# Folding the fourth and fifth modulation vector onto 64 partitions, with one matmul each

## The chip, the cores and the metric

The kernel runs on one core of a Trainium2 chip. A core has a matrix engine (PE, TensorE) with its own weight loads (PEld), a vector engine (DVE, VectorE), an activation engine (ACT, ScalarE), a general engine (POOL, GpSimd) and a queue for transfers (SP, SyncE). Each works through its own list of instructions in the order in which the program wrote them; semaphores make one engine wait for another. The metric is the time of one execution on the device in microseconds. Before the change it was 435.3 us, the median of three runs (435.18 to 435.45).

## What is computed

A block with adaptive layer norm: six modulation vectors of 448 numbers come from one small product, and shift, scale and gate a linear attention and a token-mixing MLP. Shapes: S = 2048 tokens, D = 448 channels, F = 1792, 16 heads of 28.

```python
mod = (_silu(c) @ w_mod).reshape(c.shape[0], 6, 1, -1)
sa, ca, ga, sb, cb, gb = (mod[:, 0], mod[:, 1], mod[:, 2], mod[:, 3], mod[:, 4], mod[:, 5])
h = _layernorm(x, axis=-1) * (1 + ca) + sa
x = x + ga * _A_ref(h, A_wqkv, A_wo)        # linear attention: phi(q), sums of phi(k) v, divided by den
h = _layernorm(x, axis=-1) * (1 + cb) + sb
x = x + gb * _B_ref(h, B_w1, B_b1, B_w2, B_b2)   # MLP over the token axis
```

The fourth vector is `sb`, the shift of the second layer norm (number 3 in the code, which counts from 0), the fifth is `cb`, its scale (number 4). Both are needed from the second stage on only.

## The kernel before

The 2048 tokens are 16 tiles of 128. In the first stage (the loop over `t` at L674) each tile gets its projection to keys, `phi` of it (`pk`), a copy of the normalised input (`xn`, split into a high half `xh` on ACT and a low half `xl` on DVE), and products of both that PE adds up in four banks (`cacc`). Numbers of full precision go through PE as a high and a low half, so most products are three matmuls; the high half is a copy on ACT, the low half a subtraction on DVE that waits for it (`split`, L83). Behind the loop the sums are closed: `zp` from the summed `pk` (L784), `csum` (`cs`, L794 to L796) from `cacc`, `kvb` from that and the value weights (L805), `kvm` (L809), then `wp` (L955), which PE multiplies from `kvm`. The second stage (L975) runs over the tiles once more: the transposes `tq` of the normalised queries `pn` are its first work on PE, and later `b_norm1_a` and `b_norm1_b` (L905, L909) read the fifth and the fourth vector. Pieces of the MLP's weights are loaded all along (`pr`, L316) and split into `ph` (ACT) and `pl` (DVE), two or four at a time, by `split_to` at places written out by hand. The schedule is manual: each engine gets its instructions in the order of the code.

A modulation vector is made from four blocks of `w_mod` with 112 rows each. `mod_part` (L228) scales one block by `silu(c)` and adds it to `acc`, a tile of 112 partitions by 448; what is left to do is the sum over the partitions, which is one product with ones on PE (`mod_sum2`, L256), whose result stands on all 128 partitions. `acc` has full precision, so it goes through PE in two halves. There are two ways: `split` makes two tiles of 112 partitions, `mh` and `ml`, and `mod_sum2` two matmuls; or, for the vectors named in `FOLDED`, `halves` (L236) first adds partitions 64 to 111 to 0 to 47, so that 64 are left, and then puts the high half on partitions 0 to 63 and the low half on 64 to 127 of one tile, for which one matmul does. The third and sixth vector are folded; the fourth and fifth go the first way, in `mod_split(4)` and `mod_split(3)` at L787 and L788, right behind `zb`. Their matmuls stand at L800, ahead of `kvb`, and at L811, behind it; `mod_out` copies the result to `mods`.

Of the kernel before, what the change touches and what calls it, by code (L numbers as in the profile page):

```python
# [8 lines left out]
F32 = mybir.dt.float32  # L9
# [9 lines left out]
G = 112  # L19
# [22 lines left out]
WARM = 6  # L42
POOL_LOW = (0, 2)
PRE = 9
FOLDED = (2, 5,)
MID = 5
NSLOT, NTOK = 74, 27
LOAD2, SPLIT2 = 12, 4
# [4 lines left out]
def block_kernel(ctx: ExitStack, tc: tile.TileContext, x, xt, wqkv, wo, w1, b1, w2, b2, c, wmod, wfirst, out):  # L53
    nc = tc.nc
# [22 lines left out]
    def moving(new, name, dt=F32R, parts=P):  # L77
        return new(name, dt=dt, parts=parts, w=512)[:, 16:16 + D]

    def bank(name):  # L80
        return psum.tile([P, 512], F32, name=name, tag="bank")

    def split(full, hi, lo):  # L83
        nc.scalar.activation(hi, full, AF.Copy)  # L84
        nc.vector.tensor_sub(lo, full, hi.bitcast(F32))  # L85
# [114 lines left out]
    mods, macc = {}, {}  # L200
# [32 lines left out]
            nc.vector.scalar_tensor_tensor(macc[j], wm[j, k], sc[:G, k:k + 1], macc[j], op0=ALU.mult, op1=ALU.add)  # L233


    def halves(acc, new, name):  # L236
        n = acc.shape[0] - 64
        nc.vector.tensor_add(acc[:n], acc[:n], acc[64:])
        both = moving(new, name)
        nc.scalar.activation(both[:64], acc[:64], AF.Copy)  # L240

        def low():
            nc.vector.tensor_sub(both[64:], acc[:64], both[:64].bitcast(F32))
        return both, low

    def mod_split(j):
        acc = macc.pop(j)
        if j in FOLDED:
            both, low = halves(acc, slot, f"mh{j}")
            low()  # L250
            macc[j] = (both,)
        else:
            macc[j] = (moving(slot, f"mh{j}", parts=G), moving(slot, f"ml{j}", parts=G))
            split(acc, *macc[j])

    def mod_sum2(j):  # L256
        ps = bank(f"modp{j}")
        part = macc.pop(j)
        for i, m in enumerate(part):
            nc.tensor.matmul(ps[:, :D], ones_r[:m.shape[0], :], m, start=(i == 0), stop=(i == len(part) - 1))  # L260
        return ps
# [28 lines left out]
    def row_sum(j):  # L290
        rowb[j] = bank(f"rowb{j}")
        ws = [Whi[j, ch] for ch in range(4)] + [Wlo[j, ch] for ch in range(3)]
        for i, w in enumerate(ws):
            nc.tensor.matmul(rowb[j][:ROWS, :D], sel_s, w, start=(i == 0), stop=False)

    def row_bias(j):
        nc.tensor.matmul(rowb[j][:ROWS, :D], sel_b, accb.pop(j), start=False, stop=True)
# [10 lines left out]
    raws, parts = {}, {}  # L308
# [17 lines left out]
    def split_to(i):  # L326
        while done["split"] < min(i, len(pieces)):
            k = done["split"]
            new = tslot if k in TOKP else slot
            hi, lo = new(f"ph{k}", dt=F32R, w=512), new(f"pl{k}", dt=F32R, w=512)  # L330
            if k in PIECE_DMA:
                full = raws.pop(k)
                nc.scalar.activation(hi, full, AF.Copy)
                nc.scalar.activation(lo, hi.bitcast(F32), AF.Copy, scale=-1.0)
                low_dma.append((lo, full))
            else:
                split(raws.pop(k), hi, lo)
            parts[k] = (hi, lo)
            done["split"] += 1
# [60 lines left out]
    def a_rows(t):  # L400
        g, r = groups.pop(t)[:, :, 0:2], rowst[t // 2 % RING].rearrange("p (t b c) -> p t b c", t=2, b=2)
        nc.vector.tensor_copy(r[:, :, :, 0:2], g.unsqueeze(2).to_broadcast([P, 2, 2, 2]))

        def low():
            nc.vector.tensor_sub(r[:, :, 0, 2:4], g, r[:, :, 0, 0:2].bitcast(F32))
        return low
# [6 lines left out]
    def a_copy(t):  # L413
        nc.scalar.activation(heads[t][1][64:ROWS, 384:], tps.pop(t), AF.Copy)
# [26 lines left out]
    def project(t, j, name):  # L441
        projects([(t, kind, ch) for ch in range(3) for kind in ("hh", "wl", "hl")] + [(t, "hh", 3)], j, name)

    def close(t, j):
        ps = pps.pop((t, j))
        nc.tensor.matmul(ps[:, :D], heads[t][1][:ROWS, 384:], Wrow[j][:ROWS], start=False, stop=True)  # L446
        return ps[:, :D]
# [23 lines left out]
    def phi_q(t):  # L471
        dst, (e, r) = slot(f"pq{t}"), eqs.pop(t)
        nc.vector.scalar_tensor_tensor(dst, e, 1.0, r, op0=ALU.min, op1=ALU.add)
        return dst
# [4 lines left out]
    def a_q(t):  # L479
        project(t, 0, "qp")  # L480
        qps[t] = close(t, 0)
        del heads[t]

    def a_exp_q(keep=0):
        for t in sorted(qps)[:len(qps) - keep]:
            q_exp(qps.pop(t), t)

    def a_phi_q(keep=0):
        a_exp_q(keep)
        for t in sorted(eqs):  # L490
            pq[t] = phi_q(t)
# [135 lines left out]
    low = a_rows(2)  # L627
# [18 lines left out]
    low = a_rows(4)  # L646
# [20 lines left out]
    low = a_rows(6)  # L667
# [6 lines left out]
    for t in range(4, NT):  # L674
        if 5 < t < NT - 1:
            project(t + 1, 1, "kp")
        kp = close(t, 1) if t > 4 else kps[4]
        if t == 9:
            row_sum(0)
            row_bias(0)  # L680
        if t > 4:
            a_outer(t - KV_LAG)
        if t % 2 and 4 < t < NT - 2:
            a_transpose(t + 1)
        if t in Q_EARLY:
            a_q(Q_EARLY[t])
        if t == 12:
            mp = mod_sum2(2)
        pair = t % 2 and 7 < t + 3 < NT
        if pair:  # L690
            first, second, end = a_stats_dve((t + 3, t + 4))
            first(0)
        if 5 <= t < 9:
            w_low(0, t - 5)
        if pair:
            second(0)
        if 5 <= t < 9:
            row_part(0, t - 5)
        a_phi_q(t in Q_EARLY)
        if t == 9:  # L700
            a_exp(t, kp)
        if t % 2 and 4 < t < NT - 2:
            a_copy(t + 1)
            a_copy(t + 2)
        if t != 9:
            a_exp(t, kp)
        if 7 < t + 3 < NT:
            a_split_high(t + 3)
        a_pk_parts(t - 1)
        highs = HIGH_AT.get(t, (t - 2,))  # L710
        for i in highs[:1]:
            a_norm(i)
            a_high(i)
        if t % 2 == 0 and 4 < t < NT - 3:
            low = a_rows(t + 2)
        a_pk(t, kp)
        if t % 2 == 0 and 4 < t < NT - 3:
            low()
        if 7 < t + 3 < NT:
            a_split_low(t + 3)  # L720
        for i in highs[1:]:
            a_norm(i)
            a_high(i)
        if pair:
            first(1)
        for i in highs:
            a_low(i)
        if pair:
            second(1)
            end()  # L730
        sum_end()
        if 4 <= t < 8:
            w_high(0, t - 4)
            if t == 7:
                w_row(0)
        if t == 9:
            row_out(0)
        if t == 12:
            mod_out(2, mp)
            make_mask()  # L740
        if t in FETCH:
            load_xt(FETCH[t])
            load_x(FETCH[t])
        if 7 <= t < 11:
            mod_part(2, t - 7)
        if t == 11:
            mod_split(2)
        for j, i in MOD_AT.get(t, ()):
            mod_part(j, i)
        if t in (7, 10):  # L750
            load_mod(4 if t == 7 else 3)
        if t == 10:
            load_qkv(2, tslot)
        if t == 8:
            for g in range(4):
                w = tslot(f"wo{g}", parts=G)
                nc.sync.dma_start(w, wo[g * G:(g + 1) * G, :])
                wo_sb.append(w)
            b1c = cst.tile([P, NF], F32, name="b1c")
            nc.sync.dma_start(b1c, b1)  # L760
            b2c = cst.tile([P, NT], F32, name="b2c")
            nc.sync.dma_start(b2c, b2)
        if t >= 13:
            nc.vector.tensor_mul(wo_sb[t - 13], wo_sb[t - 13], mods[2][:G])
        load_to(PRE_LOAD.get(t, 0))
# [18 lines left out]
        nc.tensor.matmul(zp[:, :D], ones_r, pk, start=(i == 0), stop=(i == 1))  # L784
    zb = tslot("zb")
    nc.scalar.activation(zb, zp[:, :D], AF.Copy, bias=S * 1e-6)
    mod_split(4)  # L787
    mod_split(3)  # L788
    load_to(14)
    split_to(4)  # L790
    a_q(late.pop(0))
    csum = []
    for ch in range(4):
        csum.append(slot(f"cs{ch}"))  # L794
        nc.scalar.activation(csum[ch], cacc[ch][:, :D], AF.Identity, scale=col[1][:, ch:ch + 1])
        nc.vector.scalar_tensor_tensor(csum[ch], zb, col[0][:, ch:ch + 1], csum[ch], op0=ALU.mult, op1=ALU.add)  # L796
    a_phi_q()
    a_q(late.pop(0))
    split_to(6)
    mp = mod_sum2(4)  # L800
    kvb = bank("kvb")
    for ch in range(4):
# [5 lines left out]
    kvm = slot("kvm", parts=G)  # L808
    nc.vector.tensor_mul(kvm, kvb[:G, :D], mask)  # L809
    mod_out(4, mp)  # L810
    mp = mod_sum2(3)  # L811
    load_to(PRE + MID + 3)
    split_to(8)
    Wpr, Wph, Wpl = [], [], []
# [133 lines left out]
            del parts[k]  # L948

    a_q(late.pop(0))  # L950
    for fn in (b_prod, b_sum, b_eps, b_recip, b_scale):
        fn(0)
    for g in range(4):
# [21 lines left out]
    for i in range(NT + LAG):  # L975
# [15 lines left out]
        t = i - LAG  # L991
# [9 lines left out]
        if i == NT:  # L1001
            mp = mod_sum2(5)
# [266 lines left out]
    for o0, n in W1G[1:]:  # L1269
# [5 lines left out]
        for r in range(first, NT):  # L1275
# [5 lines left out]
            if xleft:  # L1281
                t = xleft.pop(0)
# [81 lines left out]
```

## Time and profile before

| | |
|---|---|
| median of the runs | 435.3 us |
| the profiled execution, its own time | 435.4 us |
| its span, from first to last instruction | 433.7 us |
| granted clock of TensorE | 1.000 |
| last loop pass of the first stage, sums, start of the second stage | about 76 to 112 us |

All times below are microseconds from the start of the span. A timeline row has the start, the duration, the engine, the line, the operation, the output and inputs by their names in the program (without the tile's number), the shapes, the count of merged instructions and, in brackets, how long the engine was idle before it and what ended that. PE's matmuls overlap: their durations are longer than the distance from start to start, and it is that distance that counts.

### The profile page before, as it was taken

The page shows a single profiled execution, that of the slowest core. Times are in us where ns is not written, and L with a number is a line of the kernel's source. Part 1 is how long each engine was busy: PE and PEld are TensorE (multiplying, and loading weights), DVE is VectorE, ACT ScalarE, POOL GpSimd, SP SyncE. Part 2 cuts the span into 40 slices and gives each one's busy share as a digit, 9 for nine tenths or more (in the row PEclk, how much of TensorE's full clock was granted, in tenths as well). Part 3 has the DMA queues.
Part 4 walks back from the last instruction along what each step waited for, and adds up shares of the span by engine and source line. Part 5 has one row for each costly group of instructions (what it writes and reads, how often), then busy time and mean ns, then how long its engine had stood idle before and what let it go on. Part 6 is the DMA issues. An engine that isn't in the chain of part 4 may idle for free.

```text
span 433.7 us, 7208 instructions
## 1 busy us (share of the span) xinstructions
PE 428.1 (99%) x2333; PEld 395.5 (91%) x2333; DVE 362.2 (84%) x813; ACT 278.5 (64%) x595; POOL 119.6 (28%) x198
## 2 busy tenths in 40 slices
PE   8999999999999999999999999999999999999996
PEld 7788899999899989989999999999999999999996
DVE  4999987689799999996579695739799998898893
ACT  5899868658578799985855263537464664645550
POOL 2336444300025577775200000010113131122010
PEclk9999999999999999999999999999999999999999
DMA  8998996574200036345427461587479977886430
GB/s 278 384 334 179 242 249 152 107 225 164 86 1 0 26 73 148 73 98 121 147 85 241 144 212 50 167 209 201 85 181 215 228 157 153 218 176 125 82 54 32
DMA packets 63941, 66.14 MB, mean 152 GB/s; under 512 B 4960, under 2 KB 55456, under 8 KB 63904
## 3 DMA queue, kind: packets, MB, share of 16 engines
q1 hardware_dynamic: 54832, 50.90, 37.8%
q0 software_dynamic: 8784, 14.32, 21.1%
q10 hardware_dynamic: 288, 0.46, 0.5%
q8 instruction: 18, 0.29, 0.3%
q14 instruction: 19, 0.16, 0.1%
HBM read 46.30 MB, written 7.34 MB: 124 GB/s over the span
## 4 chain that ended last, share of the span: by engine, by line
PE 92%; DVE 4%; DMA 2%; issue 0%; POOL 0%; ACT 0%; SPq 0%; DVEq 0%
PE y L1159 19%; PE up L939 10%; PE up L938 10%; PE up L940 10%; PE y L1160 9%; PE cacc L551 8%; PE qp L439 7%; PE op L881 6%; PE kp L439 5%; PE tq L851 1%; PE op L888 1%; DMA wr<-in_qkv_dram 1%; DMA xt<-in_xt_dram 1%; PE qp L446 1%; PE kvb L805 1%; PE wp L955 1%
## 5 line engine op out<-in xcount | busy, mean ns | idle before, releaser
L939 PE MATMUL up<-h2l,ph 128*128 128x448 f32 x224 | 81.3, 363 | 0.0
L938 PE MATMUL up<-h2h,ph 128*128 128x448 f32 x224 | 81.2, 362 | 0.0
L940 PE MATMUL up<-h2h,pl 128*128 128x448 f32 x224 | 80.8, 361 | 0.0
L1114 POOL DMA_DIRECT2D a<-a x16 | 14.2, 962 | 137.8 <-DMA a<-in_B_w_dram 77.6
L938 PEld LDWEIGHTS up<-h2h,ph 128*128 128x128 f32 x224 | 42.0, 188 | 3.2
L940 PEld LDWEIGHTS up<-h2h,pl 128*128 128x128 f32 x224 | 41.9, 187 | 3.0
L939 PEld LDWEIGHTS up<-h2l,ph 128*128 128x128 f32 x224 | 42.0, 188 | 2.6 <-DVE h2l L935 0.3
L85 DVE TENSOR_TENSOR pl<-pr,ph 128x512 fp32r<-128x512 f32 x46 | 30.8, 688 | 4.1 <-ACT ph L84 3.3
L1165 ACT ACTIVATE cc<-y 128x448 f32<-128x448 f32 x24 | 13.0, 546 | 26.8 <-PE y L1160 26.8
L84 ACT ACTIVATE ph<-pr 128x512 fp32r<-128x512 f32 x46 | 27.6, 623 | 0.8 <-PE up L940 0.5
L1078 DVE TENSOR_TENSOR u<-u,mod 128x448 f32<-128x448 f32 x14 | 8.7, 623 | 21.7 <-ACT u L1077 21.5
L1077 ACT ACTIVATE u<-up,b1c 128x448 f32<-128x448 f32 x14 | 8.8, 625 | 24.1 <-PE up L940 23.5
L1179 POOL DMA_DIRECT2D out_dram<-yt x14 | 12.7, 908 | 40.8 <-DVE yt L1170 31.4
L439 PE MATMUL kp<-wh,hh 128*128 128x448 f32 x64 | 23.7, 375 | 0.0
L551 PE MATMUL cacc<-pkh,xh 128*128 128x448 f32 x64 | 23.6, 369 | 0.0
L439 PE MATMUL qp<-wh,hh 128*128 128x448 f32 x64 | 23.4, 366 | 0.0
L831 POOL TENSOR_SCALAR den<-den 128x16 f32<-128x16 f32 x16 | 8.8, 549 | 45.4 <-DVE den L828 45.4
L551 PE MATMUL cacc<-pkl,xh 128*128 128x448 f32 x56 | 20.3, 362 | 0.0
L881 PE MATMUL op<-wph,pth 128*128 128x448 f32 x48 | 18.7, 390 | 0.0
L1120 DVE TENSOR_TENSOR a<-a,s 128x512 f32<-128x512 f32 (+1 forms) x32 | 18.5, 622 | 0.0
L84 ACT ACTIVATE s2h<-s 128x512 fp32r<-128x512 f32 (+1 forms) x16 | 8.3, 569 | 15.5 <-DVE s L1120 15.5
L1159 PE MATMUL y<-ub,a11h 128*128 128x448 f32 x56 | 18.2, 375 | 0.0
(239 smaller groups left out, 1378.1 us busy)
## 6 DMA issues: line engine op xcount, KB each, us to landing
pr<-in_B_w_dram SPq DMA_DIRECT2D x56, 256.0 KB, 3.1
a<-in_B_w_dram SPq DMA_DIRECT2D x32, 256.0 KB, 4.4
a<-in_B_w_dram SPq DMA_DIRECT2D x32, 192.0 KB, 4.2
xt<-in_xt_dram SPq DMA_DIRECT2D x16, 256.0 KB, 5.0
x<-in_A_x_dram SPq DMA_DIRECT2D x16, 224.0 KB, 5.0
wm<-in_B_wmod_dram SPq DMA_DIRECT2D x16, 196.0 KB, 5.4
out_dram<-x SPq DMA_DIRECT2D x14, 224.0 KB, 2.2
out_dram<-yt POOLq DMA_DIRECT2D x14, 224.0 KB, 5.7
```

What stands on the lines that cost most here:

```text
L84: nc.scalar.activation(hi, full, AF.Copy)
L85: nc.vector.tensor_sub(lo, full, hi.bitcast(F32))
L439: nc.tensor.matmul(pps[t, j][:, :D], a[:, ch * P:(ch + 1) * P], w, start=first, stop=False)
L551: nc.tensor.matmul(cacc[ch][:, :D], a[:, s], b, start=(t == 0 and i == 0), stop=(t == NT - 1 and i == len(todo) - 1))
L881: nc.tensor.matmul(opb[t][:, :D], a, b, start=(ch == n == 0), stop=False)
L938: nc.tensor.matmul(ps[:, :D], hi[:, sl], mh, start=first, stop=False)
L939: nc.tensor.matmul(ps[:, :D], hi[:, sl], ml, start=False, stop=False)
L940: nc.tensor.matmul(ps[:, :D], lo[:, sl], mh, start=False, stop=last)
L1114: nc.gpsimd.dma_start(w, a, accum_op=ALU.add)
L1120: nc.vector.tensor_tensor(w, raw2[q, a][i], raw2[q, b][i], op=op)
L1159: nc.tensor.matmul(ps[:, :D], h[:, s], w, start=opens and r == 0, stop=False, skip_group_check=True)
L1160: nc.tensor.matmul(ps[:, :HD], l[:, s], wh, start=False, stop=closes and r == PAIRS - 1, skip_group_check=True)
```

## The change

Both vectors are folded now. `halves` is cut into three steps, `mod_add`, `mod_high` and a low half that is called by itself, so that they can stand at different places. For the fifth vector, add and high half are written at the end of tile 13 in the loop of the first stage, the low half at the end of tile 14; for the fourth the add stands behind `csum`, the high half behind the second projection there, and the low half behind the next pair of weight pieces. The fifth vector's sum stays ahead of `kvb`; the fourth's moves behind it and behind the next projection, ahead of `wp`.

```diff
-FOLDED = (2, 5,)
...
-    def halves(acc, new, name):
-        n = acc.shape[0] - 64
-        nc.vector.tensor_add(acc[:n], acc[:n], acc[64:])
-        both = moving(new, name)
+    def mod_add(j):
+        acc = macc[j]
+        nc.vector.tensor_add(acc[:G - 64], acc[:G - 64], acc[64:])
+
+    def mod_high(j):
+        acc, both = macc[j], moving(slot, f"mh{j}")
+        macc[j] = (both,)
         nc.scalar.activation(both[:64], acc[:64], AF.Copy)
-
-        def low():
-            nc.vector.tensor_sub(both[64:], acc[:64], both[:64].bitcast(F32))
-        return both, low
+        return lambda: nc.vector.tensor_sub(both[64:], acc[:64], both[:64].bitcast(F32))

     def mod_split(j):
-        acc = macc.pop(j)
-        if j in FOLDED:
-            both, low = halves(acc, slot, f"mh{j}")
-            low()
-            macc[j] = (both,)
-        else:
-            macc[j] = (moving(slot, f"mh{j}", parts=G), moving(slot, f"ml{j}", parts=G))
-            split(acc, *macc[j])
+        mod_add(j)
+        mod_high(j)()
...
+        if t == 13:
+            mod_add(4)
+            low4 = mod_high(4)
+        if t == 14:
+            low4()
...
-    mod_split(4)
-    mod_split(3)
     load_to(14)
     split_to(4)
     a_q(late.pop(0))
...
+    mod_add(3)
     a_phi_q()
     a_q(late.pop(0))
+    low3 = mod_high(3)
     split_to(6)
+    low3()
     mp = mod_sum2(4)
...
     mod_out(4, mp)
-    mp = mod_sum2(3)
...
     a_q(late.pop(0))
+    mp = mod_sum2(3)
     for fn in (b_prod, b_sum, b_eps, b_recip, b_scale):
```

Where the instructions stand, at the two places of which the prediction speaks. The lines of the changed kernel are other ones than before; in the names the number right behind the letters is the tile's, the vector's or the piece's, the one behind the underscore a running number.

ACT at the end of tile 13, before the change (`xh` of tiles 11 and 12, then the exponentials for the query of tile 3, `eq3`, and the key of tile 14):

```order
L503 ACTIVATE xh11_1169<-xn11_1167 128x448
L503 ACTIVATE xh12_1176<-xn12_1174 128x448
L468 ACTIVATE eq3_1222<-qp3_1138,mv2_334 128x448
L469 ACTIVATE rq3_1223<-qp3_1138,mv2_334 128x448
L453 ACTIVATE ek14_1228<-kp14_1113,mv14_993 128x448
L456 ACTIVATE rk14_1229<-kp14_1113,mv14_993 128x448
L519 ACTIVATE pkh13_1232<-pk13_1172 128x448
```

and now:

```order
L496 ACTIVATE xh11_1169<-xn11_1167 128x448
L496 ACTIVATE xh12_1176<-xn12_1174 128x448
L242 ACTIVATE mh4_1185<-acc4_872 64x448
L461 ACTIVATE eq3_1225<-qp3_1138,mv2_334 128x448
L462 ACTIVATE rq3_1226<-qp3_1138,mv2_334 128x448
L446 ACTIVATE ek14_1231<-kp14_1113,mv14_993 128x448
L449 ACTIVATE rk14_1232<-kp14_1113,mv14_993 128x448
L512 ACTIVATE pkh13_1235<-pk13_1172 128x448
```

The fifth vector's high half, `mh4`, stands between `xh12` and `eq3`, and everything behind it in the list comes after it. DVE at the same place, before (low halves of tiles 11 and 12, then the first part of the fourth vector):

```order
L509 TENSOR_TENSOR xl11_1170<-xn11_1167,xh11_1169 128x384
L508 TENSOR_TENSOR xh12_1176<-xn12_1174,xh12_1176 128x64
L509 TENSOR_TENSOR xl12_1177<-xn12_1174,xh12_1176 128x384
L231 TENSOR_SCALAR acc3_1184<-wm3_0_940,sc_194 112x448
L764 TENSOR_TENSOR wo0_784<-wo0_784,mod2_1107 112x448
L473 SCALAR_TENSOR_TENSOR pq3_1226<-eq3_1222,rq3_1223 128x448
L521 SCALAR_TENSOR_TENSOR pkl13_1233<-pk13_1172,pkh13_1232 128x448
```

and now:

```order
L502 TENSOR_TENSOR xl11_1170<-xn11_1167,xh11_1169 128x384
L501 TENSOR_TENSOR xh12_1176<-xn12_1174,xh12_1176 128x64
L502 TENSOR_TENSOR xl12_1177<-xn12_1174,xh12_1176 128x384
L237 TENSOR_TENSOR acc4_872<-acc4_872 48x448
L230 TENSOR_SCALAR acc3_1187<-wm3_0_940,sc_194 112x448
L762 TENSOR_TENSOR wo0_784<-wo0_784,mod2_1107 112x448
L466 SCALAR_TENSOR_TENSOR pq3_1229<-eq3_1225,rq3_1226 128x448
L514 SCALAR_TENSOR_TENSOR pkl13_1236<-pk13_1172,pkh13_1235 128x448
```

The add on `acc4` stands behind `xl12`; `mh4` on ACT reads its result. The low half of the fifth vector stands one tile later on DVE, behind `xl13`:

```order
L502 TENSOR_TENSOR xl13_1243<-xn13_1240,xh13_1242 128x384
L243 TENSOR_TENSOR mh4_1185<-acc4_872,mh4_1185 64x448
L232 SCALAR_TENSOR_TENSOR acc3_1187<-wm3_1_942,sc_194,acc3_1187 112x448
L762 TENSOR_TENSOR wo1_786<-wo1_786,mod2_1107 112x448
L466 SCALAR_TENSOR_TENSOR pq4_1272<-eq4_1268,rq4_1269 128x448
L514 SCALAR_TENSOR_TENSOR pkl14_1279<-pk14_1245,pkh14_1278 128x448
```

Before, `acc3` followed `xl13` there directly. Behind the sums, ACT before (from the exponentials of tile 5's query, over the third pair of weight pieces, to the copy of the fifth vector):

```order
L468 ACTIVATE eq5_1430<-qp5_1406,mv4_413 128x448
L469 ACTIVATE rq5_1431<-qp5_1406,mv4_413 128x448
L84 ACTIVATE ph4_1448<-pr4_1310 128x512
L84 ACTIVATE ph5_1452<-pr5_1312 128x512
L468 ACTIVATE eq6_1476<-qp6_1436,mv6_486 128x448
L469 ACTIVATE rq6_1477<-qp6_1436,mv6_486 128x448
L204 ACTIVATE mod4_1484<-modp4_1456 128x448
```

and now:

```order
L461 ACTIVATE eq5_1427<-qp5_1402,mv4_413 128x448
L462 ACTIVATE rq5_1428<-qp5_1402,mv4_413 128x448
L242 ACTIVATE mh3_1445<-acc3_1187 64x448
L83 ACTIVATE ph4_1447<-pr4_1314 128x512
L83 ACTIVATE ph5_1451<-pr5_1316 128x512
L461 ACTIVATE eq6_1475<-qp6_1433,mv6_486 128x448
L462 ACTIVATE rq6_1476<-qp6_1433,mv6_486 128x448
L203 ACTIVATE mod4_1483<-modp4_1456 128x448
```

The fourth vector's high half, `mh3`, stands ahead of the pieces `ph4` and `ph5`; before, both vectors had their high halves right behind `zb`, ahead of the second pair of pieces and of `csum`. DVE there before, from the two low halves that went with them to `pq6`, behind which comes `kvm`:

```order
L85 TENSOR_TENSOR ml4_1383<-acc4_872,mh4_1382 112x448
L85 TENSOR_TENSOR ml3_1387<-acc3_1184,mh3_1386 112x448
L85 TENSOR_TENSOR pl2_1399<-pr2_1296,ph2_1398 128x512
L85 TENSOR_TENSOR pl3_1403<-pr3_1298,ph3_1402 128x512
L796 SCALAR_TENSOR_TENSOR cs0_1418<-zb_1380,col0_199,cs0_1418 128x448
L796 SCALAR_TENSOR_TENSOR cs1_1421<-zb_1380,col0_199,cs1_1421 128x448
L796 SCALAR_TENSOR_TENSOR cs2_1424<-zb_1380,col0_199,cs2_1424 128x448
L796 SCALAR_TENSOR_TENSOR cs3_1427<-zb_1380,col0_199,cs3_1427 128x448
L473 SCALAR_TENSOR_TENSOR pq5_1434<-eq5_1430,rq5_1431 128x448
L85 TENSOR_TENSOR pl4_1449<-pr4_1310,ph4_1448 128x512
L85 TENSOR_TENSOR pl5_1453<-pr5_1312,ph5_1452 128x512
L473 SCALAR_TENSOR_TENSOR pq6_1480<-eq6_1476,rq6_1477 128x448
```

and now:

```order
L84 TENSOR_TENSOR pl2_1395<-pr2_1300,ph2_1394 128x512
L84 TENSOR_TENSOR pl3_1399<-pr3_1302,ph3_1398 128x512
L792 SCALAR_TENSOR_TENSOR cs0_1414<-zb_1384,col0_199,cs0_1414 128x448
L792 SCALAR_TENSOR_TENSOR cs1_1417<-zb_1384,col0_199,cs1_1417 128x448
L792 SCALAR_TENSOR_TENSOR cs2_1420<-zb_1384,col0_199,cs2_1420 128x448
L792 SCALAR_TENSOR_TENSOR cs3_1423<-zb_1384,col0_199,cs3_1423 128x448
L237 TENSOR_TENSOR acc3_1187<-acc3_1187 48x448
L466 SCALAR_TENSOR_TENSOR pq5_1431<-eq5_1427,rq5_1428 128x448
L84 TENSOR_TENSOR pl4_1448<-pr4_1314,ph4_1447 128x512
L84 TENSOR_TENSOR pl5_1452<-pr5_1316,ph5_1451 128x512
L243 TENSOR_TENSOR mh3_1445<-acc3_1187,mh3_1445 64x448
L466 SCALAR_TENSOR_TENSOR pq6_1479<-eq6_1475,rq6_1476 128x448
```

`ml4` and `ml3` are gone from ahead of `cs0`; the add on `acc3` stands behind `cs3`, and the low half, into `mh3`, behind `pl5`; `kvm` follows `pq6` as before.

## Prediction

> **What bounds the kernel now.** I read the page's busy times first, then the waits of PE (TensorE), then the windows around the two places that the change touches, then the timelines of PE, DVE (VectorE) and ACT (ScalarE) there.
>
> ```profile
> PE 428.1 (99%) x2333; PEld 395.5 (91%) x2333; DVE 362.2 (84%) x813; ACT 278.5 (64%) x595; POOL 119.6 (28%) x198
> ...
> PE warm L189 <- DVE roots L109: 1.1, 1, 1.1
> ...
> PE tq L851 <- DVE pn L838: 0.2, 1, 0.2
> ...
> 92.00:112.00 20.00, 20.00 (x112) 17.30 (x111) 18.56 (x34) 13.58 (x27) 0.29 (x1) 1.00 0.55 179
> 112.00:202.00 90.00, 89.72 (x471) 82.83 (x470) 82.90 (x196) 71.80 (x165) 51.91 (x95) 1.00 0.31 68
> ```
>
> PE is busy for 99% of the span, and its waits (total, times, longest) are some tenths of a microsecond behind the start-up. Nothing but PE sets the time, so a matmul less is worth its pitch and a microsecond for which PE stands still is a microsecond lost. The second window is the warning: from 92 to 112 us DVE is busy for 18.56 of 20 us (third figure behind PE and PEld). What is put on DVE there finds little idle time.
>
> **PE's own work.**
>
> ```profile
> 102.43 0.36 PE L260 MATMUL modp<-mh,ones_r 112*128 112x448 f32 x1
> 102.64 0.37 PE L260 MATMUL modp<-ml,ones_r 112*128 112x448 f32 x1
> 102.84 3.40 PE L805 MATMUL kvb<-cs,wr 128*112 128x112 f32 x32
> ...
> 106.49 0.37 PE L439 MATMUL qp<-wh,hh 128*128 128x448 f32 x1
> ...
> 108.70 3.17 PE L955 MATMUL wp<-wo,kvm 112*112 112x448 f32 x8
> 111.70 0.49 PE L851 MATMUL tq<-ident,pn 128*128 128x128 f32 x3
> ```
>
> Each vector now takes one matmul instead of two. Start to start a modp matmul takes 0.20 (102.43, 102.64, 102.84), so two of them give **-0.40 us**. That is all that PE can gain, as there is no wait of PE here that could go too.
>
> **What a fold costs DVE and ACT.** The third vector is folded already; its rows show the price of add, high half and low half.
>
> ```profile
> 68.84 0.17 DVE L393 TENSOR_SCALAR ve<-mv 128x4 f32<-128x4 f32 x1
> 69.04 0.62 DVE L238 TENSOR_TENSOR acc<-acc 48x448 f32<-48x448 f32 x1
> 70.30 0.62 DVE L243 TENSOR_TENSOR mh<-acc,mh 64x448 fp32r<-64x448 f32 x1 [0.65 <-ACT mh L240]
> 70.95 0.69 DVE L233 SCALAR_TENSOR_TENSOR acc<-wm,sc,acc 112x448 f32<-112x448 f32 x1
> ...
> 69.69 0.58 ACT L240 ACTIVATE mh<-acc 64x448 fp32r<-64x448 f32 x1 [1.71 <-DVE acc L238]
> 70.18 0.61 ACT L468 ACTIVATE eq<-qp,mv 128x448 f32<-128x448 f32 x1
> ```
>
> Fewer partitions are not cheaper: the 48x448 add takes 0.62. ACT starts 0.03 behind the add's end, its next instruction 0.49 behind that, and DVE's next 0.65 behind the low half. The add starts 0.03 after its neighbour's end (68.84 + 0.17 = 69.01), while most DVE rows start some 0.08 before it. I take the 0.03 for all four added instructions; with the usual overlap each would be 0.11 cheaper, 0.45 in all, and that is one bound. The Trainium skill, page "VectorE: DVE Perf Modes", section "Two Vector instructions with no wait between them", says that a Vector instruction whose operands start in another group of 32 partitions than the last one's starts only when all earlier ones have finished. By that rule all four are held, which is the sum below; without it the sum would be 437.7, and the rows at 69.04 and 70.95 side with the rule.
>
> **Tile 13, the fifth vector.** On ACT the high half now stands between tile 12's `xh` and `eq3`; it waits for the add, which stands on DVE behind tile 12's `xl`.
>
> ```profile
> 80.47 1.03 ACT L503 ACTIVATE xh<-xn 128x448 fp32r<-128x448 f32 x2
> 81.40 0.62 ACT L468 ACTIVATE eq<-qp,mv 128x448 f32<-128x448 f32 x1
> ...
> 83.47 0.59 ACT L519 ACTIVATE pkh<-pk 128x448 fp32r<-128x448 f32 x1
> 85.71 0.58 ACT L503 ACTIVATE xh<-xn 128x448 fp32r<-128x448 f32 x1 [1.65 <-DVE xn L499]
> ...
> 81.81 0.55 DVE L509 TENSOR_TENSOR xl<-xn,xh 128x384 fp32r<-128x384 f32 x1
> ...
> 84.09 0.63 DVE L521 SCALAR_TENSOR_TENSOR pkl<-pk,pkh 128x448 fp32r<-128x448 f32 x1 [0.30 <-ACT pkh L519]
> ...
> 86.47 0.55 DVE L509 TENSOR_TENSOR xl<-xn,xh 128x384 fp32r<-128x384 f32 x1
> 86.93 0.68 DVE L233 SCALAR_TENSOR_TENSOR acc<-wm,sc,acc 112x448 f32<-112x448 f32 x1
> ...
> 89.31 0.63 DVE L521 SCALAR_TENSOR_TENSOR pkl<-pk,pkh 128x448 fp32r<-128x448 f32 x1 [0.63 <-ACT pkh L519]
> ```
>
> `xl` ends at 82.36; add 82.39 to 83.01; high half 83.04; `eq3` 83.53 instead of 81.40: **ACT is 2.13 late**, 1.64 of it waiting. Behind `eq3` four instructions follow without a gap to `pkh` at 83.47, DVE waits for `pkh` (84.09), and ACT waits for DVE again (85.71). ACT's 1.65 idle there is one leg of this round trip and absorbs nothing, so tile 13's `xl` starts at 88.60 and ends at 89.15. The low half (tile 14 in the program) follows at 89.18, `acc` at 89.83 instead of 86.93: 2.90 late. The idle 0.63 at 89.31 (0.71 with the overlap) takes some back: `pkl` of tile 14 at 91.50, **2.19 late**, and so the chain runs on to the sums.
>
> **When PE feels it.**
>
> ```profile
> 90.94 0.58 ACT L503 ACTIVATE xh<-xn 128x448 fp32r<-128x448 f32 x1 [1.65 <-DVE xn L499]
> ...
> 91.91 0.55 DVE L509 TENSOR_TENSOR xl<-xn,xh 128x384 fp32r<-128x384 f32 x1
> ...
> 96.23 0.62 DVE L85 TENSOR_TENSOR zl<-pk,zh 128x448 fp32r<-128x448 f32 x1 [0.70 <-ACT zh L84]
> ...
> 93.22 0.36 PE L551 MATMUL cacc<-pkh,xh 128*128 128x448 f32 x1
> ...
> 93.62 0.36 PE L551 MATMUL cacc<-pkh,xl 128*128 128x448 f32 x1
> ...
> 97.82 0.36 PE L784 MATMUL zp<-zl,ones_r 128*128 128x448 f32 x1
> ```
>
> From an operand's end to its matmul I count 0.12, as at the first `kvb` (102.10 + 0.62 to 102.84, rows here and below). With 2.19 more, `xh` of tile 14 is there at 93.83 (needed 93.22, PE loses 0.61), `xl` at 94.77 (needed 93.62; 1.15 in all), `zl` at 99.16 (needed 97.82; **1.34** in all).
>
> **Behind the sums, the fourth vector.**
>
> ```profile
> 99.83 1.16 DVE L85 TENSOR_TENSOR ml<-acc,mh 112x448 fp32r<-112x448 f32 x2
> ...
> 102.10 2.47 DVE L796 SCALAR_TENSOR_TENSOR cs<-zb,col,cs 128x448 f32<-128x448 f32 x4
> ...
> 105.02 1.29 DVE L85 TENSOR_TENSOR pl<-pr,ph 128x512 fp32r<-128x512 f32 x2
> ...
> 106.88 0.63 DVE L809 TENSOR_TENSOR kvm<-kvb,mask 112x448 f32<-112x448 f32 x1
> ...
> 110.60 0.62 DVE L838 SCALAR_TENSOR_TENSOR pn<-pq,den 128x448 f32<-128x448 f32 x1
> ...
> 103.74 1.18 ACT L84 ACTIVATE ph<-pr 128x512 fp32r<-128x512 f32 x2
> ```
>
> The two `ml` go, 1.07 of DVE (99.83 to the next start at 100.90). So `cs` starts at 102.10 + 2.19 - 1.07 = 103.22, and its first tile is good for a matmul at 103.96; PE arrives at 102.84 + 1.34 - 0.20 = 103.98, in step. `qp7` follows at +0.74 (the second matmul is gone), and `wp` could start at 108.70 + 0.74 + 0.20 = 109.64, the fourth vector's single matmul standing before it now. But the four `cs` end at 105.69; the add runs from 105.72 to 106.34; ACT has meanwhile waited for it, starts the high half at 106.37 and `ph4` at 106.86, 3.12 late. DVE's `pl4` waits for that (106.86 + 0.66, so 107.55), the pair of `pl` ends at 108.84, low half 108.87, `pq6` 109.52, `kvm` at about 110.1, 3.2 late. `wp` starts at 110.8. Nothing waits on ACT or POOL in between that was not there before, so `pn` keeps the 3.2: it starts at 113.8, and `tq` of tile 0 at 114.5 instead of 111.70: **+2.8 us** in all, with the 0.40 taken off. From 112 on PE is busy for 89.72 of 90 us, so no idle time is left to give it back.
>
> The queue of loads keeps its order, but tiles come from one pool, and the first piece `pr0` now takes a slot that tile 12's accumulating DMAs must leave, as `pr1` did before:
>
> ```profile
> SPq L316 <- DMA pk<-pk: 3.3, 1, 3.3
> ```
>
> That holds the loads up by those 3.3 us at most, from 82.75 to some 86; `ph0` reads the piece at 96.11, now later still. I count nothing for it.
>
> The profiled execution took 435.4 us with a span of 433.7; plus 2.8 it is 438.2. Its time lies 0.1 above the median of the runs, 435.3, so the forecast is **438.1**.
>
> **Rivals.** *Hidden, not slower:* the add is early enough for ACT to lose less than the smallest margin of PE, 0.85 at `zl` (97.82 - 96.97). Then only -0.40 is left: 434.9. For it speaks that DVE and ACT are each idle at times; against it that both work through their rows in order, and the add stands behind `xl`, which itself waits for ACT's `xh`. It decides from 0.85 us of delay on, and I count 2.19. Chance 0.06. *One place alone:* were only the fifth to cost, PE would reach `wp` at 109.64, +0.94, 436.2; were only the fourth to cost, all its terms would come 2.19 earlier and `tq` at 112.3, +0.6, 435.9. Chance 0.09. *More:* the delay of DVE grows again in the loop over the tiles behind `tq`, by up to 1 us (439.1), if a tile's `pn` waits a second time; the 0.2 wait at `tq` shows that the loop has little to spare. Against it, ACT's and DVE's work there waits for PE and moves with it. Chance 0.07. That the change does not do what it says can be left out: the built order shows one matmul for each vector.
>
> **How the numbers follow.** 0.78 for the forecast, whose own range is 437.2 (the four holds cost nothing and half a microsecond of margins was misread) to 438.7. The range 436.5 to 438.9 leaves out the hidden case, the single places and the upper part of "more", some 0.18. A measurement of this kernel tells 0.2%, 0.87 us, from no change: slower is over 436.2, faster under 434.4. Hidden and single places lie between: 0.14; slower 0.85; faster 0.01, as no row offers more than 0.40.
>
> **What would show it.** In the profile after: ACT idle for some 1.5 us before the fifth's high half, ended by the add; PE with new waits at `cacc` for tile 14's `xh` and `xl` and at `zp`; ACT idle before the fourth's high half, `kvm` at 110, and PE waiting for `kvm` at `wp` and for `pn` at `tq`, about 1.2 and 0.8 us. The forecast is wrong if PE shows no waits from 92 to 115 us, or if ACT reaches `eq3` before 82.5.

## The result and the profile after

The changed kernel takes 438.35 us (median of six runs, 438.2 to 438.98), the kernel before beside it 435.43 us. The ratio is 1.007 with a 95% interval of 1.0059 to 1.008: slower by 2.6 to 3.5 us. The profiled execution took 438.2 us, with a span of 436.5 us and a granted clock of 1.0. From the changed kernel's profile, first the busy times, then the waits of PE at the change (total, times, longest), and last the window from 92 to 112 us, whose row from before is the first of the two windows in the prediction:

```profile
PE 429.2 (98%) x2331; PEld 395.1 (91%) x2331; DVE 363.9 (83%) x815; ACT 278.6 (64%) x595; POOL 119.3 (27%) x198
```

```profile
PE wp L954 <- DVE kvm L808: 0.8, 1, 0.8
PE tq L849 <- DVE pn L836: 0.7, 2, 0.6
PE cacc L544 <- ACT xh L496: 0.5, 1, 0.5
...
PE cacc L544 <- DVE xl L502: 0.2, 1, 0.2
```

```profile
92.00:112.00 20.00, 18.54 (x101) 15.42 (x101) 18.46 (x34) 12.41 (x24) 0.00 (x0) 1.00 0.52 172
```

Four waits are new or longer: `cacc` for ACT's `xh` and DVE's `xl`, `wp` for `kvm`, `tq` for `pn`. From 92 to 112 us PE was busy without a break before and is now for 18.54 us, while DVE is as busy as it was (18.46 us against 18.56). The time sits where PE stands still, and the engine that lets it wait is not the one with much more to do.

The timelines show the path there. This execution runs 0.20 us ahead of that of before from the start-up on (ACT's pair of `xh` of tile 12 at 80.27, before at 80.47), so 0.20 is added below wherever a time is set against before. First ACT, then DVE:

```profile
80.27 1.03 ACT L496 ACTIVATE xh<-xn 128x448 fp32r<-128x448 f32 x2
82.84 0.58 ACT L242 ACTIVATE mh<-acc 64x448 fp32r<-64x448 f32 x1 [1.55 <-DVE acc L237]
83.33 0.61 ACT L461 ACTIVATE eq<-qp,mv 128x448 f32<-128x448 f32 x1
...
106.20 0.58 ACT L242 ACTIVATE mh<-acc 64x448 fp32r<-64x448 f32 x1 [2.04 <-DVE acc L237]
106.69 1.14 ACT L83 ACTIVATE ph<-pr 128x512 fp32r<-128x512 f32 x2
```

```profile
81.61 0.55 DVE L502 TENSOR_TENSOR xl<-xn,xh 128x384 fp32r<-128x384 f32 x1
82.19 0.62 DVE L237 TENSOR_TENSOR acc<-acc 48x448 f32<-48x448 f32 x1
...
89.02 0.62 DVE L243 TENSOR_TENSOR mh<-acc,mh 64x448 fp32r<-64x448 f32 x1
89.67 0.69 DVE L232 SCALAR_TENSOR_TENSOR acc<-wm,sc,acc 112x448 f32<-112x448 f32 x1
...
103.05 2.47 DVE L792 SCALAR_TENSOR_TENSOR cs<-zb,col,cs 128x448 f32<-128x448 f32 x4
105.55 0.62 DVE L237 TENSOR_TENSOR acc<-acc 48x448 f32<-48x448 f32 x1
...
109.97 0.62 DVE L808 TENSOR_TENSOR kvm<-kvb,mask 112x448 f32<-112x448 f32 x1
```

Twice ACT stands in front of a high half until DVE gets to the add (1.55 and 2.04 us), and both times work that DVE and then PE need is queued behind it: `eq` at 83.33 (83.53 on the clock of before, which had it at 81.40), `ph` at 106.69. PE then:

```profile
93.64 0.47 PE L544 MATMUL cacc<-pkh,xh 128*128 128x448 f32 x1 [0.46 <-ACT xh L496]
...
94.53 0.47 PE L544 MATMUL cacc<-pkh,xl 128*128 128x448 f32 x1 [0.21 <-DVE xl L502]
...
98.92 0.47 PE L782 MATMUL zp<-zl,ones_r 128*128 128x448 f32 x1
...
110.64 3.26 PE L954 MATMUL wp<-wo,kvm 112*112 112x448 f32 x8 [0.78 <-DVE kvm L808]
114.46 0.52 PE L849 MATMUL tq<-ident,pn 128*128 128x128 f32 x3 [0.56 <-DVE pn L836]
```

With the 0.20, `zl` is consumed at 99.12 (before 97.82, +1.30), `wp` starts at 110.84 (108.70, +2.1) and the first `tq` at 114.66 (111.70, +2.96). Behind it nothing is regained: the whole span is 2.8 us longer, 3.0 with the 0.20.

### The profile page after: what moved, and what is told of

Same layout as the page of the kernel before. It is cut to its first block, busy times and chain, and to the rows that moved or that the text cites. A ratio compares the mean times of both kernels' runs of the same rounds, so it can differ in the third digit from the quotient of the medians.

```text
span 436.5 us, 7205 instructions
## 1 busy us (share of the span) xinstructions
PE 429.2 (98%) x2331; PEld 395.1 (91%) x2331; DVE 363.9 (83%) x815; ACT 278.6 (64%) x595; POOL 119.3 (27%) x198
## 4 chain that ended last, share of the span: by engine, by line
PE 86%; DVE 9%; DMA 2%; issue 1%; ACT 1%; POOL 0%; SPq 0%; DVEq 0%; ACTq 0%
PE y L1158 19%; PE up L937 10%; PE up L936 10%; PE up L938 10%; PE y L1159 9%; PE qp L432 6%; PE op L879 6%; PE cacc L544 6%; PE kp L432 5%; PE tq L849 1%; PE op L886 1%; DMA wr<-in_qkv_dram 1%; DMA xt<-in_xt_dram 1%; PE kp L439 1%; DVE pl L84 1%
```

## The experiments

All ran on the chip beside the kernel before, whose median there was 435.6 us. **Theory T** is that of the prediction: two places, at each of which ACT waits in its order for an add that stands late in DVE's order. **Rival W** holds the added work itself responsible, wherever it stands. Differences in us are (ratio - 1) x 435.6. Four of these kernels leave out a part of the two vectors' sums: add_aside, no_shift, no_shift_beside and one_matmul; they serve for their times alone.

| run | median, us | ratio to before, 95% interval | us |
|---|---|---|---|
| changed_again | 438.75 | 1.0065 (1.0052 to 1.0078) | +2.8 |
| fifth_alone | 437.26 | 1.0037 (1.0024 to 1.0049) | +1.6 |
| fourth_alone | 436.95 | 1.0029 (1.0018 to 1.0041) | +1.3 |
| add_aside | 436.49 | 1.0019 (1.001 to 1.0027) | +0.8 |
| high_later | 436.89 | 1.0028 (1.0019 to 1.0037) | +1.2 |
| in_the_gap | 436.37 | 1.0014 (1.0005 to 1.0023) | +0.6 |
| fourth_in_gap | 436.55 | 1.0023 (1.0014 to 1.0032) | +1.0 |
| **both_in_gaps** | **434.98** | **0.9985 (0.9976 to 0.9993)** | **-0.7** |
| one_matmul | 435.35 | 0.9994 (0.9985 to 1.0003) | -0.3 |
| no_shift | 438.15 | 1.005 (1.0038 to 1.0063) | +2.2 |
| no_shift_beside | 437.84 | 1.0045 (1.0031 to 1.0059) | +2.0 |

### One vector at a time

The first run returns the fourth vector to the split on 112 partitions, the second the fifth. For the first (the second likewise, with `j == 4` and the old call of `mod_split(4)`):

```diff
     def mod_split(j):
+        if j == 3:
+            acc = macc.pop(j)
+            macc[j] = (moving(slot, f"mh{j}", parts=G), moving(slot, f"ml{j}", parts=G))
+            split(acc, *macc[j])
+            return
         mod_add(j)
         mod_high(j)()
...
+    mod_split(3)
     load_to(14)
...
-    mod_add(3)
     a_phi_q()
     a_q(late.pop(0))
-    low3 = mod_high(3)
     split_to(6)
-    low3()
...
+    mp = mod_sum2(3)
     load_to(PRE + MID + 3)
...
-    mp = mod_sum2(3)
```

> The changed kernel, but only the fifth vector is folded (tiles 13 and 14); the fourth is split on 112 partitions and takes two matmuls at its old place. Baselines: 435.4 before, 438.35 changed. Theory T (both places cost, by engines that wait in order): the 2.19 us by which DVE is late at the sums stays; of the two ml subtractions one goes (0.53), so cs starts at 102.10 + 2.19 - 0.53 = 103.76 and the first kvb matmul, 0.74 behind that, at 104.50, where the kernel before had 102.84: +1.66, nothing is added behind it, so about 437.0, with PE waiting at cacc, zp and kvb and no longer at wp. Rival W (what counts is the work that DVE and ACT got, not the waiting): DVE's busy time grew by 1.7 us in all, half of it is here, about 436.3. Rival 4 (only the fourth vector's place costs): 435.2. Rival 5 (only the fifth's place costs): 438.3.

> The changed kernel, but only the fourth vector is folded (behind the sums with the shift, its matmul behind wp); the fifth is split on 112 partitions and takes two matmuls. Theory T: nothing is late up to the sums; one ml goes, so cs runs from 101.57 to 104.04, the add ends at 104.69, the high half starts at 104.72, ph at 105.21 instead of 103.74, pl, the low half and pq6 follow, kvm starts at about 108.4 instead of 106.88; PE waits about 0.6 at wp and again at tq, +1.2 there: 436.6. Both places alone then come to +1.6 and +1.2, which adds up to the +2.9 of the two together. Rival W: half of the added work, 436.3. Rival 4: 438.3. Rival 5: 435.2.

Measured: +1.6 and +1.3, where T gave +1.6 and +1.2. Both rivals that name one place alone (-0.2 for the other place) are out, and the two sum to the whole. W's 436.3, which is +0.9 or a ratio of 1.0021 against the 435.4 it was written for, is outside the first interval and inside the second; these two runs alone don't settle it. PE's waits moved as T said, except that none is listed at `zp`; first with the fifth alone, then with the fourth alone:

```profile
PE cacc L549 <- ACT xh L501: 0.5, 1, 0.5
PE kvb L807 <- DVE cs L798: 0.3, 1, 0.3
```

```profile
PE tq L850 <- DVE pn L837: 0.7, 2, 0.6
PE wp L955 <- DVE kvm L809: 0.7, 1, 0.7
```

### The same work, without the wait

Here the add writes to partitions that ACT does not read, so that ACT no longer waits for it; every instruction stays in its place in the order.

```diff
-        nc.vector.tensor_add(acc[:G - 64], acc[:G - 64], acc[64:])
+        dst = acc[64:] if j in (3, 4) else acc[:G - 64]
+        nc.vector.tensor_add(dst, acc[:G - 64], acc[64:])
```

> The changed kernel, but the two additions (fourth and fifth vector) write their sum to rows 64 to 111 of the accumulator instead of rows 0 to 47, so that ACT's high half no longer waits for them: DVE and ACT run the same instructions in the same order. It leaves out the share of rows 64 to 111 in these two vectors. Theory T: the 1.64 us of ACT's waiting at tile 13 and the 2.0 behind the sums go, eq3 starts at about 81.8 instead of 83.33, PE has no wait at cacc and zp and nearly none at wp; by the order of the instructions with the durations of before, tq of tile 0 comes at +0.6: 436.0. Rival W (the work itself costs): no change, 438.35.

Measured: +0.8, T's +0.6 within the interval (+0.4 to +1.2) and W's +2.8 far outside. So some 2.0 of the 2.8 us is ACT's waiting, and DVE and ACT did this with the busy time of the changed kernel. First the busy times and PE's waits, then ACT's timeline, in which neither row has an idle time in front:

```profile
PE 428.2 (99%) x2331; PEld 395.2 (91%) x2331; DVE 363.9 (84%) x815; ACT 278.6 (64%) x595; POOL 119.6 (28%) x198
...
PE tq L850 <- DVE pn L837: 0.7, 2, 0.6
PE wp L955 <- DVE kvm L809: 0.3, 1, 0.3
```

```profile
81.40 0.57 ACT L243 ACTIVATE mh<-acc 64x448 fp32r<-64x448 f32 x1
81.87 0.62 ACT L462 ACTIVATE eq<-qp,mv 128x448 f32<-128x448 f32 x1
```

### Other places for the fifth vector

The first run moves only ACT's high half, from the end of tile 13 to tile 14 behind `pkh`. The second puts the add behind the last accumulation at tile 12 and both halves behind `phi_q` of tile 13; there DVE was idle before for the 2.54 us ahead of `pk` (row below).

```diff
         a_pk_parts(t - 1)
+        if t == 14:
+            low4 = mod_high(4)
...
             mod_add(4)
-            low4 = mod_high(4)
```

```diff
         a_phi_q(t in Q_EARLY)
+        if t == 13:
+            mod_high(4)()
...
-        if t == 13:
-            mod_add(4)
-            low4 = mod_high(4)
-        if t == 14:
-            low4()
         for j, i in MOD_AT.get(t, ()):
             mod_part(j, i)
+        if t == 12:
+            mod_add(4)
```

> The changed kernel, but ACT's high half of the fifth vector stands at tile 14, behind pkh of tile 13, instead of in front of eq3; the addition stays where it is, and so does all that concerns the fourth vector. Theory T (ACT's waiting at tile 13 starts the delay): ACT waits for nothing there, eq3 starts at 81.5, PE has no wait at cacc and zp, and what is left is the fourth vector's place, as in the run with the fourth alone: +1.1 to +1.3 on the kernel before. Rival W (the added work itself costs, 0.5 us of ACT and 1.3 of DVE at this place): the fifth's share stays, +2.5 to +2.8. A hold of each DVE instruction whose rows start elsewhere stays in this run.

> The changed kernel, but the fifth vector's addition stands at the end of tile 12, behind its last accumulation, and its high and low half right behind phi_q of tile 13, where ACT and DVE both wait for PE's new product; the fourth vector as in the changed kernel. Theory T: the fold of the fifth costs nothing there; PE has no wait at cacc and zp, and the fourth's place is left, less what an earlier DVE gives back: by the order with the durations of before +0.7, at most +1.2. Rival W: +2.5 to +2.8, since the work is the same.

Measured: +1.2 and +0.6, as T has it; W's +2.5 to +2.8 is out. The difference between the two is DVE's. DVE's timeline before (the gap), then `zl` in high_later and in in_the_gap:

```profile
79.52 0.63 DVE L461 SCALAR_TENSOR_TENSOR pk<-ek,rk 128x448 f32<-128x448 f32 x1 [2.54 <-ACT rk L456]
```

```profile
96.90 0.62 DVE L84 TENSOR_TENSOR zl<-pk,zh 128x448 fp32r<-128x448 f32 x1 [0.70 <-ACT zh L83]
```

```profile
96.46 0.63 DVE L84 TENSOR_TENSOR zl<-pk,zh 128x448 fp32r<-128x448 f32 x1 [0.70 <-ACT zh L83]
```

With the high half moved, nothing waits at tile 13, but add and low half still stand in a stretch where DVE has little room: `zl` starts 0.55 later than before (96.23, and by the pair of `xh`, here at 80.59, this execution runs 0.12 late). In the gap it keeps its place (the pair at 80.70, 0.23 late, and `zl` at 96.46). Counted the same way, `wp` (109.30 and 108.86) starts 0.55 apart too.

### Both in gaps, and the fourth alone in its gap

In the first of these the fifth stands as in the run before, and of the fourth the add moves behind `pn` of tile 0 (`b_scale`), the halves behind the `wp` products and the matmul to tile 1 of the second stage; in the second the fifth stays at tiles 13 and 14. The fourth's part, the same in both:

```diff
-    mod_add(3)
     a_phi_q()
     a_q(late.pop(0))
-    low3 = mod_high(3)
     split_to(6)
-    low3()
...
-    mp = mod_sum2(3)
     for fn in (b_prod, b_sum, b_eps, b_recip, b_scale):
         fn(0)
+    mod_add(3)
...
-    mod_out(3, mp)
+    mod_high(3)()
...
+        if i == 1:
+            mp = mod_sum2(3)
         if i < NT:
             b_transpose(i)
...
+        if i == 1:
+            mod_out(3, mp)
```

> As the run with the fifth vector in the gap at tile 13, and the fourth's addition behind b_scale of tile 0, its high and low half behind the eight wp products, its matmul and mod_out at tile 1 of the second stage, where both engines have room. Theory T: no wait of PE is left that the kernel before did not have, so only the two matmuls saved count: -0.2 to -0.4, 435.2 to 435.4 where the kernel before has 435.6. Rival W: +2.5 to +2.8. Rival P (a matmul with one operand over 64 rows in place of two over 112 brings PE nothing, or the later matmul stands in PE's way): 0 to +0.3.

> The changed kernel with the fifth vector at tiles 13 and 14 as it is, and the fourth vector where the faster run has it: its addition behind b_scale of tile 0, its high and low half behind the eight wp products, its matmul at tile 1 of the second stage. This is the case 'only the fifth's place costs' with both folded. Theory T: PE has the waits at cacc and zp (1.34 in all) and reaches wp at +0.74, nothing is added there, and the later matmul takes its 0.20: +0.9, where the run with both in gaps has -0.5 and the one with only the fifth in a gap +0.6 to +0.7. Rival S (the two places are not independent: a late fifth makes DVE late up to the end of the stage, so that part of the cost shows only behind wp): +1.3 or more, with a wait at wp or tq.

Measured: -0.7 (interval -1.0 to -0.3; T's -0.4 lies in it, its -0.2 does not, and neither do Rival P's 0 to +0.3) and +1.0. The version with both in gaps is faster than either kernel, and it executes what the changed kernel executes:

```profile
PE 427.7 (99%) x2331; PEld 395.2 (91%) x2331; DVE 363.9 (84%) x815; ACT 278.7 (64%) x595; POOL 119.6 (28%) x198
```

As many instructions on DVE (815, 363.9 us) and ACT (595) as in the changed kernel, 3.5 us apart: W is out, and the place makes the cost. PE's timeline in this run:

```profile
108.18 3.17 PE L950 MATMUL wp<-wo,kvm 112*112 112x448 f32 x8
111.18 0.49 PE L845 MATMUL tq<-ident,pn 128*128 128x128 f32 x3
118.14 0.37 PE L253 MATMUL modp<-mh,ones_r 128*128 128x448 f32 x1
118.35 0.60 PE L845 MATMUL tq<-ident,pn 128*128 128x128 f32 x4
```

No new wait; the first `tq` is 0.52 earlier than before (in an execution that runs 0.15 late by its pair of `xh`), and the later `modp` takes its 0.20 ahead of the second.

With the fourth alone in its gap, PE's path is the prediction's "only the fifth": `wp` at 109.33 in an execution 0.13 early, so +0.76, with no wait there:

```profile
109.33 3.17 PE L951 MATMUL wp<-wo,kvm 112*112 112x448 f32 x8
```

The four cases side by side: both in gaps -0.7, the fourth alone at its place of the change +0.6, the fifth alone +1.0, both +2.8. Counted from -0.7, the single places cost 1.3 and 1.7, and both 3.5; the 0.5 that is left over is less than the width of any of these intervals (0.7 to 1.1), so the runs don't tell whether the places add up exactly. In the prediction's own sums they do not: counted from -0.40, its +0.94 and +0.6 for single places are 1.3 and 1.0, and its +2.8 for both is 3.2, as two delays spend PE's margin (0.85 at `zl`) only once. (In fifth_alone the fifth gives +1.6 rather than +1.0, because there the fourth's `ml` still stands ahead of `cs`, for which PE waits at `kvb`, and because one matmul less is saved. That fifth_alone and fourth_alone sum to the whole therefore doesn't show that the places add up.) Rival S asked for +1.3 or more with a new wait at `wp` or `tq`: the interval reaches to +1.4, but the waits did not come.

### What PE gains by itself

This is the kernel before, without the matmul of the low half for these two vectors.

```diff
-        part = macc.pop(j)
+        part = macc.pop(j)[:1]
```

> The kernel before, with the matmul of the high half alone for the fourth and fifth vector; all of DVE's and ACT's work stays. It leaves out the low halves of these two vectors. It prices what PE saves by itself: two pitches of 0.20 us, -0.3 to -0.4. If PE's order gives nothing (the wait at tq, 0.2, grows by as much), 0.

Measured: -0.3, with an interval (-0.7 to +0.1) that holds 0 as well as -0.40; the run's time does not decide, the timeline does:

```profile
102.96 0.37 PE L260 MATMUL modp<-mh,ones_r 112*128 112x448 f32 x1
103.36 3.40 PE L805 MATMUL kvb<-cs,wr 128*112 128x112 f32 x32
106.53 0.45 PE L260 MATMUL modp<-mh,ones_r 112*128 112x448 f32 x1
```

`kvb` starts 0.40 behind the only `modp`, where 0.20 is the pitch: it now waits for `cs`, whose timing did not change. Only the second vector's 0.20 arrives. In the folded kernels `cs` comes earlier, since the two `ml` of 1.07 us are gone from in front of it, and there both pitches can count: in both_in_gaps `cs` starts at 101.19 and `kvb` at 102.80, which with that execution's 0.15 is 1.06 and 0.19 earlier than before.

### The four added DVE instructions on rows from 0 on

Here both additions and both low halves read and write partitions from 0 on alone; order and waits stay. A shifted instruction is one of which an operand starts at another partition, here at 64.

```diff
-        nc.vector.tensor_add(acc[:G - 64], acc[:G - 64], acc[64:])
+        src = acc[:G - 64] if j in (3, 4) else acc[64:]
+        nc.vector.tensor_add(acc[:G - 64], acc[:G - 64], src)
...
+        if j in (3, 4):
+            macc[j] = (both[:64],)
+            return lambda: nc.vector.tensor_sub(both[:64], acc[:64], both[:64].bitcast(F32))
```

> The changed kernel, but the four added DVE instructions read and write rows from 0 on alone (the addition adds rows 0 to 47 to themselves, the low half stands in place of the high half, and the matmul goes over 64 rows), with all waits as they are. It leaves out rows 64 to 111 and the high halves of these two vectors. Theory T with the holds (an instruction whose rows start elsewhere starts 0.03 behind its neighbour's end instead of 0.08 before it, 0.11 each, 0.45 in four): DVE's added rows start before their neighbours' ends, and the time is 437.9. Rival (no hold, the start depends on something else): the rows start 0.03 behind as before and the time stays at 438.35.

> The changed kernel itself, beside the others on one chip: 2.8 to 2.9 over the kernel before.

> The changed kernel with the four added DVE instructions on rows from 0 on alone, once more beside the changed kernel itself (it leaves out rows 64 to 111 and the high halves of these two vectors). Four holds of 0.11 give 0.45 less than the changed kernel. Rival: the instruction behind each shifted one is held too, as the rows of the profile (one start 0.03 behind its neighbour's end ahead of the shifted instruction and one behind it) suggest, eight holds of 0.10, of which the idle time in front of pkl of tile 14 and of the pair pl takes some back: 0.6 to 0.8 less.

Measured side by side: 437.84 against 438.75, 0.9 less; the first time +2.2, 0.6 below changed_again's +2.8. The intervals overlap, so these times alone don't separate 0.45 from the rival's 0.6 to 0.8, and the size is taken from the rows. DVE's timeline in no_shift_beside, then in changed_again:

```profile
82.41 0.55 DVE L506 TENSOR_TENSOR xl<-xn,xh 128x384 fp32r<-128x384 f32 x1
82.88 0.61 DVE L238 TENSOR_TENSOR acc<-acc 48x448 f32<-48x448 f32 x1
83.41 0.44 DVE L230 TENSOR_SCALAR acc<-wm,sc 112x448 f32<-112x448 f32 x1
...
110.04 0.62 DVE L812 TENSOR_TENSOR kvm<-kvb,mask 112x448 f32<-112x448 f32 x1
```

```profile
82.18 0.55 DVE L502 TENSOR_TENSOR xl<-xn,xh 128x384 fp32r<-128x384 f32 x1
82.76 0.62 DVE L237 TENSOR_TENSOR acc<-acc 48x448 f32<-48x448 f32 x1
83.42 0.45 DVE L230 TENSOR_SCALAR acc<-wm,sc 112x448 f32<-112x448 f32 x1
...
110.55 0.62 DVE L808 TENSOR_TENSOR kvm<-kvb,mask 112x448 f32<-112x448 f32 x1
```

Without the shift the add starts 0.08 before the end of `xl` (82.88 against 82.96), and the next instruction 0.08 before the add's end. With it the add starts 0.03 behind, and the next 0.04 behind. So each shifted instruction costs twice, once in front and once behind. From `xl` to `kvm` it is 28.37 against 27.63 us: 0.74 in all, not 0.45, as the rival has it. What the add's follower loses does not get that far, since DVE waits for ACT soon after; the 0.74 is the other six, some 0.12 each.

## Why the prediction was right, and where a price in it was not

The forecast was 438.1 us and slower; 438.35 came. Step by step, on the clock of before:

- **PE's -0.40** stands, with a condition that the prediction had only in its arithmetic (`cs` 1.07 earlier): without the folding's relief of DVE, half of it is lost (one_matmul, by its rows), with it and no wait the kernel gains 0.3 to 1.0 us (both_in_gaps).
- **Tile 13**: `eq3` was put at 83.53 and came at 83.53. The low half's follower `acc` was put at 89.83, and came at 89.87. That ACT's waiting is the main cause is shown by high_later (no wait of ACT there, `eq` in step, and of the 2.2 us between the fifth in the gap, +0.6, and at its place, +2.8, some 0.6 left, which is DVE's work where it has little room) and by add_aside, where 2.0 go with the waits; the 1.5 from there to both_in_gaps is left to the work itself at crowded places.
- **PE at the sums**: 0.61, 1.15 and 1.34 us were forecast for `xh`, `xl` and `zl`; 0.62, 1.11 and 1.30 came (93.22, 93.62 and 97.82 before). The "hidden" rival fell here: `zl` came 2.21 late on DVE, against a margin of 0.85.
- **The fourth vector**: `cs` put at 103.22, found at 103.25; add 105.72 and 105.75; high half 106.37 and 106.40; `kvm` 110.1 and 110.17; `wp` 110.8 and 110.84. `tq` was put at 114.5 and came at 114.66, 0.16 more. Half of the 0.16 is in the prediction's own sum: from `pq6` at 109.52 its rows (106.22 to 106.88) lead to `kvm` at 110.18, not 110.1.
- **The rivals' prices**: "only the fifth" at +0.9 measured +1.0 (fourth_in_gap), "only the fourth" at +0.6 measured +0.6 (in_the_gap). They held as prices of these places; they did not hold as cases of this change, in which both places cost. "More" did not come: behind `tq`, 2.96 late, the end is 3.0 late.
- **The signs** came, but for a wait at `zp`, which no row lists. PE's waits at `wp` and `tq`, named as 1.2 and 0.8, have 0.78 and 0.56 in the rows, which count from the modelled end of the matmul in front; start to start PE's delay grows by 1.24 up to `wp` (from 1.30 less the 0.40 to 2.14) and by 0.82 up to `tq`.
- **The holds** are the term that was mis-sized. The prediction said that with the usual overlap each of four instructions would be 0.11 cheaper, 0.45 in all, and 437.7 without them. The rows show the follower late as well, and 0.74 together at `kvm`, so that price should have read about 437.4. The sum itself did not suffer: it had set the followers 0.03 behind the low half and ACT's high half behind the add, as the trace did. The Trainium skill, page "VectorE: DVE Perf Modes", section "Two Vector instructions with no wait between them", holds an instruction whose operands start in another group of 32 partitions until all earlier ones are done; the rows agree (0.03 behind with the shift, 0.08 before without). That reaches the instruction behind a low half, whose output starts at another partition than the low half's; that the one behind the add is late too is told by the rows alone.

The loads of the weight pieces, which the prediction counted at nothing, began at 85.46 (85.66 on the clock of before, against 82.75), as it allowed; in the changed kernel's trace no instruction of ACT or DVE waits for one of these loads.

## What to carry to other kernels

An instruction saved on the bound engine is worth its pitch only if the operands of what follows come earlier too, and the instructions that pay for it must stand where the engines that run them are idle: the same 815 and 595 instructions gave +2.8 us in one order and -0.7 us in another. Before an engine is handed a step that waits for another engine, look up what stands behind it in its own order, and how late in the other's order the awaited step comes. The price is that lateness, less the margin of the bound engine behind it (for the fifth vector 2.2 us on DVE, less 0.85 at `zl`: 1.3 at the sums), and not the step's duration. In this kernel each partition shift on DVE cost the overlap in front and the one behind.

## What the hardware showed beside this

In the gap at tile 13 the low half took longer than anywhere else. DVE's timeline in in_the_gap, POOL's beside it, and POOL's before:

```profile
77.33 0.99 DVE L243 TENSOR_TENSOR mh<-acc,mh 64x448 fp32r<-64x448 f32 x1
78.33 0.77 DVE L492 TENSOR_SCALAR xn<-x,mv 128x448 f32<-128x448 f32 x1
```

```profile
76.89 0.96 POOL L98 TENSOR_SCALAR_AFFINE_SELECT mask<-mask 112x448 f32<-112x448 f32 x1
77.92 0.93 POOL L100 TENSOR_SCALAR_AFFINE_SELECT mask<-mask 112x448 f32<-112x448 f32 x1
```

```profile
76.69 0.83 POOL L99 TENSOR_SCALAR_AFFINE_SELECT mask<-mask 112x448 f32<-112x448 f32 x1
77.59 0.67 POOL L101 TENSOR_SCALAR_AFFINE_SELECT mask<-mask 112x448 f32<-112x448 f32 x1
```

The subtraction takes 0.99 instead of 0.62, the `xn` behind it 0.77 instead of 0.51, and POOL's two selects beside them take 0.96 and 0.93 instead of 0.83 and 0.67; both_in_gaps shows the same 0.99. Both engines lose when they meet there, in a gap wide enough to hide it. As `xn` has no shift and is slower too, the shift alone does not explain it. The Trainium skill, page "SBUF — State Buffer", section "SBUF: two separate sides", says that DVE and GpSimd share a pair of ports, and that of a DVE instruction with two inputs from SBUF and a GpSimd one that reads SBUF the first to start holds the pair for its whole length while the other blocks. The rows fit a contention in kind, but they show no clean block: the subtraction, begun 0.44 behind the first select, ends 0.47 behind it, in less than its 0.62. No run here separated this from another cause.
